# Attention and feed-forward on one core: output product five units behind, weights two pieces an iteration, interleaved tables, a mean in column groups, and a later test

## The chip, the cores and the metric

The kernel runs on one core of a Trainium2 chip. The metric is the device time of one execution in microseconds (us), the median of several. A profile's *span* is the time from the first to the last instruction; here it lies some 1.7 to 2.2 us below the time of the same execution.

## The reference

A linear attention with decay (RWKV-5) over 4 batches, 8 heads, 768 steps, head size 48, followed by a feed-forward block with SoLU and a layer norm. Cut to what matters:

```python
# attention, for every step t
y[:, :, t] = einsum('bhd,bhde->bhe', rt, state + (u*kt) vt)
state = w * state + kt vt
# feed-forward on x = y as (3072, 384); w_in is 384 x 1024, w_out 1024 x 384
h    = x @ w_in
solu = h * softmax(h)
ln   = (solu - mean(solu)) / sqrt(var(solu) + 1e-6) * g_ln
out  = ln @ w_out
```

The feed-forward weights arrive as 64-bit floats; the kernel converts them to 32-bit in 14 pieces (6 of `w_in`, 8 of `w_out`).

## The kernel before

The work is cut into 24 units of 128 rows, (batch, chunk). One loop runs a software pipeline over them, in an order that the program fixes for every engine. In iteration `i` unit `i + 2` is turned (`tr`, `tk`), unit `i + 1` gets its scores (`at`), unit `i` its attention output and state update (`y`, `kv`), unit `i - 2` its first feed-forward product (`h`) and SoLU (`solu`), and unit `l` is turned (`t`) and multiplied with `w_out` (`o`). Before the change `l = i - 5`, that is `LA, LO = 2, 3`.

Instead of subtracting the mean from every row, the kernel subtracts the column mean from `w_out` once (`centre`), so `o` of the first unit must wait for all of `w_out`. While it runs it tests that the decays and the sums of Exp lie in a safe range; a small matrix product (`n_ps`) adds the results up, and a branch at the end redoes all in another way if the test failed.

Short names in what follows: `rku` is the product of r, k and u, and `own` its sum per head; `kp` is k weighted with the decay; rT, kT and lnT are the turned r, k and `solu` after their copy out of PSUM (the memory that TensorE writes; the kernel shares it out in banks), and xT is the copy of the attention output `y`.

```python
    for j in range(7):                                   # tables, one after the other
        nc.vector.tensor_mul(pw[:, 0, j + 1], pw[:, 0, j], pw[:, 0, j])
    double(0)                                            # 7 products: decay backward
    ...                                                  # kdec from it, then
    nc.vector.reciprocal(out=pw[:, 1], in_=pw[:, 0])
    nc.vector.tensor_copy(out=fore[:, :, T - 1 : T], in_=pw[:, 1, 0].unsqueeze(2))
    double(1)                                            # 7 products: its inverse
    ...
    def column_mean(fs):                                 # mean over the rows of w_out
        for f in fs:
            nc.tensor.matmul(mean[0], ones, w_out_sb[:, f, :], start=(f == 0), stop=(f == KF - 1), ...)
            if f == KF - 1:
                nc.scalar.copy(out=mean_sb, in_=mean[0])
    ...
    conversions = {-2: 1, -1: 1, 0: 2, 1: 2, 2: 3, 3: 3, 4: 2}
    for i in range(-2, N + LA + LO):
        j, l = i - LA, i - LA - LO
        ...                     # turn_r, sum_own, turn_k of unit i + 2
        ...                     # convert_d of the last pieces; convert_a, convert_b of this iteration's
        if i + 3 < N:
            decay_k(i + 3)      # kp, on GpSimd
        for p in now:
            convert_c(p)        # adds the low words, on GpSimd
        if i + 3 < N:
            weigh(i + 3, nc.gpsimd)   # rku
        ...
        if 0 <= j < N:
            ffn_in(j)           # h, Exp
        if l == 0:
            column_mean(fs); centre(...) ; turn_ln(l)
        if 0 <= i + 1 < N:
            scores(i + 1)       # at, masked copy
        if 0 <= j < N:
            unit(j)             # solu, Square, statistics
        if i == N + LA - 1:
            check_sums()        # n_ps
        if i + 2 < N:
            diagonal(i + 2)     # AT, on ScalarE
        ...                     # t, o, then y, kv, xT of unit i
```

## Time and profile before

| | before |
|---|---|
| median time | 432.87 us (432.8 to 433.84) |
| span of the profile | 431.2 us |
| TensorE busy | 400.3 us, 93% |
| end of the first `solu` | 51.57 us |
| `h` of iteration 6 starts | 98.96 us in the timeline (99.13 in the chain) |
| a steady iteration, from `h` to `h` | 16.08 us, all of it TensorE work |

In the profile PE is TensorE, PEld its weight load, DVE VectorE, ACT ScalarE, POOL GpSimd. A line of a timeline has the start, the duration, engine, source line, operation, output and inputs, shapes and count, and in brackets how long the engine stood idle before it and what ended that. The chain of work that ended last has start, duration and what ran. The prediction below shows the lines of before and how to read them.

### The profile page before, as it was taken

The numbers are of one execution on the slowest core, as the hardware profiler recorded it, in microseconds if no ns is written. First come the engines' busy times: TensorE is split into PE (matmuls) and PEld (weight loads), VectorE is DVE, ScalarE is ACT, GpSimd is POOL, SyncE is SP. The second block draws the span as 40 slices with busy tenths as digits, with TensorE's granted clock in tenths as the row PEclk, the third lists the DMA queues.
The fourth block names the chain that finished last, engine by engine and source line by source line (L and its number), as shares of the span: only waits on it lengthen the run. The fifth ranks groups of instructions, "written<-read, shape, count | busy, mean of one in ns | idle before, by whom it ended". The sixth has DMA issues, their size and how long they took to land.

```text
span 431.2 us, 7237 instructions
## 1 busy us (share of the span) xinstructions
PE 400.3 (93%) x2871; PEld 252.9 (59%) x2871; DVE 158.2 (37%) x303; ACT 181.3 (42%) x423; POOL 145.2 (34%) x220
## 2 busy tenths in 40 slices
PE   2689598999999999999999999999999999998895
PEld 1576355565665665665665665665665665554562
DVE  6787965373224226224224224233233132111200
ACT  1776268633552552552552452452452452323211
POOL 4587644763513513513414414414413011001100
PEclk9998889999999999999999999999999999999898
DMA  8998990003403303303303303302300000000011
GB/s 167 282 215 188 184 117 5 2 0 75 74 6 69 74 14 63 73 17 60 73 20 56 73 22 55 73 24 52 73 20 1 20 20 1 20 20 19 2 38 43
DMA packets 81593, 25.93 MB, mean 60 GB/s; under 512 B 76557, under 2 KB 79758, under 8 KB 81550
## 3 DMA queue, kind: packets, MB, share of 16 engines
q1 hardware_dynamic: 81406, 25.18, 29.1%
q8 instruction: 24, 0.39, 0.4%
q10 hardware_dynamic: 144, 0.20, 0.1%
q14 instruction: 19, 0.16, 0.1%
HBM read 20.65 MB, written 4.72 MB: 59 GB/s over the span
## 4 chain that ended last, share of the span: by engine, by line
PE 79%; DVE 10%; ACT 4%; POOL 2%; issue 2%; DMA 1%; ACTq 0%; POOLq 0%; DVEq 0%; SPq 0%
PE o_ps L817 29%; PE h_ps L774 25%; PE y_ps L744 7%; PE t_ps L806 5%; PE at L716 5%; PE kv_ps L760 4%; DVE ma L524 2%; PE tk_ps L705 2%; PE tr_ps L697 2%; DVE ma L526 2%; ACT AT L691 2%; DVE mag L520 1%; DVE tab L575 1%; DVE w_out_sb L663 1%; POOL rku L680 1%
## 5 line engine op out<-in xcount | busy, mean ns | idle before, releaser
L774 PE MATMUL h_ps<-w_in_sb,xT 128*128 128x512 f32 x288 | 130.1, 602 | 5.1 <-DVE solu L786 5.1
L817 PE MATMUL o_ps<-w_out_sb,lnT 128*128 128x384 f32 x384 | 130.8, 495 | 1.0 <-DVE lnT L808 1.0
L817 PEld LDWEIGHTS o_ps<-w_out_sb,lnT 128*128 128x128 f32 x384 | 72.0, 192 | 49.6 <-issue 3.3
L774 PEld LDWEIGHTS h_ps<-w_in_sb,xT 128*128 128x128 f32 x288 | 53.8, 194 | 64.2 <-issue 64.2
L719 DVE COPY_PREDICATED AT<-later,at 128x512 f32<-128x512 uint32 x48 | 32.1, 721 | 94.8 <-ACT e L777 94.8
L777 ACT ACTIVATE e<-h_ps 128x1024 f32<-128x1024 f32 x24 | 24.5, 1023 | 93.8 <-PE h_ps L774 93.8
L691 ACT ACTIVATE AT<-ident,own 128x128 f32<-128x128 f32 x192 | 58.4, 386 | 4.5 <-DVE own L685 4.5
L789 ACT ACTIVATE sq<-solu 128x1024 f32<-128x1024 f32 x24 | 25.4, 1057 | 76.6 <-DVE solu L786 76.6
L791 POOL TENSOR_TENSOR st<-st 128x1 f32<-128x1 f32 x24 | 4.6, 193 | 149.9 <-DVE solu L786 149.9
L716 PEld LDWEIGHTS at<-rT,kT 48*128 48x128 f32 x384 | 25.7, 199 | 19.0 <-issue 15.7
L763 DVE TENSOR_TENSOR state<-kv_ps,state 128x384 f32<-128x384 f32 x16 | 8.9, 558 | 74.5 <-PE kv_ps L760 74.5
L764 POOL TENSOR_TENSOR state<-state,wt 128x384 f32<-128x384 f32 x16 | 16.1, 1006 | 51.1 <-DVE state L763 51.1
L716 PE MATMUL at<-rT,kT 48*128 48x128 f32 x384 | 30.8, 298 | 2.5 <-DVE AT L719 2.4
L674 POOL TENSOR_TENSOR kp<-kpad,kdec 128x512 f32<-128x512 f32 x24 | 31.2, 1302 | 5.5 <-ACT kdec L591 5.4
L786 DVE SCALAR_TENSOR_TENSOR solu<-h_ps,st,e 128x1024 f32<-128x1024 f32 x24 | 30.8, 1284 | 1.0
L808 DVE COPY lnT<-t_ps 128x512 f32<-128x512 f32 x24 | 16.4, 684 | 30.2 <-PE t_ps L806 30.0
L744 PE MATMUL y_ps<-AT,vt 128*32 128x128 f32 x768 | 27.2, 285 | 0.0
L806 PE MATMUL t_ps<-ident,solu 128*128 128x128 f32 x192 | 25.6, 277 | 0.2 <-ACT xT L756 0.2
L706 ACT COPY kT<-tk_ps 128x512 f32<-128x512 f32 x24 | 14.0, 583 | 24.9 <-PE tk_ps L705 24.8
L760 PE MATMUL kv_ps<-vt,kp 128*128 128x96 f32 x160 | 24.2, 298 | 0.0
L681 POOL TENSOR_TENSOR rku<-rku,rpad 128x384 f32<-128x384 f32 x23 | 22.9, 997 | 1.8
L820 ACT ACTIVATE o<-o_ps,st 128x384 f32<-128x384 f32 x24 | 13.6, 566 | 23.6 <-PE o_ps L817 15.1
(77 smaller groups left out, 375.0 us busy)
## 6 DMA issues: line engine op xcount, KB each, us to landing
kpad<-in_k_dram SPq DMA_DIRECT2D x24, 192.0 KB, 3.4
rpad<-in_r_dram SPq DMA_DIRECT2D x24, 192.0 KB, 4.1
vt<-in_v_dram SPq DMA_DIRECT2D x24, 192.0 KB, 4.0
out_dram<-o SPq DMA_DIRECT2D x24, 192.0 KB, 2.0
raw<-in_moe_w_in_dram SPq DMA_DIRECT2D x6, 512.0 KB, 5.6
raw<-in_moe_w_out_dram SPq DMA_DIRECT2D x8, 384.0 KB, 3.4
u_bc<-in_u_dram ACTq DMA_DIRECT2D x1, 192.0 KB, 3.7
wq<-in_w_dram SPq DMA_DIRECT2D x1, 1.5 KB
```

The lines of the kernel that those rows point to most:

```text
L674: nc.gpsimd.tensor_mul(X["kp"].rearrange("p h d -> p (h d)"), kpads[i % NLD].rearrange("p h d -> p (h d)"), kdec.rearrange("p a d -> p (a ...
L691: nc.scalar.activation(out=AT[:, h, :], in_=ident, func=ACT.Copy, scale=X["own"][:, h])
L716: nc.tensor.matmul(pss[q][:, a, :], X["kT"][rows, a, :], X["rT"][rows, a, :], start=True, stop=True)
L719: nc.vector.copy_predicated(A4[:, :, q, :], later.to_broadcast([128, HP, T]), pss[q])
L744: nc.tensor.matmul(y_ps[32 * g : 32 * g + 32, j, :], lhsT, rhs, start=(g not in opened), stop=stop, skip_group_check=True)
L760: nc.tensor.matmul(kv_ps[:, a], pair(X["kp"], a), vt[:, 2 * a : 2 * a + 2, 0:D], start=True, stop=True)
L774: nc.tensor.matmul(h_ps[:, ts(n, NX)], X["xT"][:, j, :], w_in_sb[:, j, ts(n, NX)], start=(j == 0), stop=(j == KD - 1))
L777: nc.scalar.activation(out=e, in_=h_ps, func=ACT.Exp, accum_out=sums[:, i : i + 1])
L786: nc.vector.scalar_tensor_tensor(out=solu, in0=X["h"], scalar=rs, in1=X["e"], op0=ALU.mult, op1=ALU.mult, accum_out=tot)
L789: nc.scalar.activation(out=sq, in_=solu, func=ACT.Square, accum_out=ss)
L806: nc.tensor.transpose(t_ps[:, f, :], X["solu"][:, ts(4 * g + f, 128)], ident)
L817: nc.tensor.matmul(o_ps, X["lnT"][:, f, :], w_out_sb[:, f, :], start=(f == 0), stop=(f == KF - 1))
```

## The change

Its intent: to empty the head of the kernel, where TensorE waits for the weight conversion, and the tail, where it waits for the test. The output product falls two units further behind, so that the 14 pieces can be spread at two an iteration; the two tables grow together; `rku` of the first units stands ahead of the weight addition on GpSimd; the column mean is summed in four groups of 32 columns, which needs a second product to add the groups; Square writes over `e`; and the test goes to the very end. The diff, cut to its core:

```diff
-    LA, LO = 2, 3
+    LA, LO = 2, 5
...
-    for j in range(7):
-        nc.vector.tensor_mul(pw[:, 0, j + 1], pw[:, 0, j], pw[:, 0, j])
-    double(0)
+    for j in range(8):
+        if j < 7:
+            nc.vector.tensor_mul(pw[:, 0, j + 1], pw[:, 0, j], pw[:, 0, j])
+            nc.vector.reciprocal(out=pw[:, 1, j], in_=pw[:, 0, j])
+        if j == 0:
+            nc.vector.tensor_copy(out=fore[:, :, T - 1 : T], in_=pw[:, 1, 0].unsqueeze(2))
+        else:
+            n = 1 << (j - 1)
+            nc.vector.tensor_mul(tab[:, :, :, T - 2 * n : T - n], tab[:, :, :, T - n : T],
+                                 pw[:, :, j - 1].unsqueeze(3).to_broadcast([128, 2, HP, n]))
...
+            nc.tensor.matmul(mean[0][ts(f % 4, 32), :], part[:, 0:32], w_out_sb[:, f, :],
+                             start=(f < 4), stop=(f >= KF - 4), skip_group_check=True)
+
+    def column_mean():
+        nc.scalar.copy(out=mean_sb, in_=mean[0])
+        ps = psM.tile([128, dm], F32, tag="m", name="mean_ps2")
+        nc.tensor.matmul(ps, part, mean_sb, start=True, stop=True)
+        nc.scalar.activation(out=mean_sb, in_=ps, func=ACT.Copy, scale=32.0 / dff)
...
-    conversions = {-2: 1, -1: 1, 0: 2, 1: 2, 2: 3, 3: 3, 4: 2}
+    conversions = {-2: 1, -1: 1, 0: 2, 1: 2, 2: 2, 3: 2, 4: 2, 5: 2}
...
             decay_k(i + 3)
+            if i < 0:
+                weigh(i + 3, nc.gpsimd)
         for p in now:
             convert_c(p)
-        if i + 3 < N:
+        if 0 <= i and i + 3 < N:
             weigh(i + 3, nc.gpsimd)
...
+        column_sums(fs)         # behind scores(i + 1)
...
-        if i == N + LA - 1:
-            check_sums()
+        if l == N - 1:          # ahead of the last output product
+            check_sums()
...
+        if 7 in fs:             # last thing in iteration 6
+            column_mean()
             for f in range(KF):
                 centre(f, nc.vector if f % 2 == 0 else nc.gpsimd)
```

Rings of `solu` and of statistics are larger to match the lag.

More of the change, by code (lines that the diff above doesn't have):

```diff
@@ L570, in direct_path @@
     nc.vector.memset(back[:, :, T - 1 : T], 1.0)
-    def double(x):
-        for j in range(7):
-            n = 1 << j
-            nc.vector.tensor_mul(tab[:, x, :, T - 2 * n : T - n], tab[:, x, :, T - n : T],
-                                 pw[:, x, j].unsqueeze(2).to_broadcast([128, HP, n]))
     wd_ps = psM.tile([128, HP], F32, tag="m", name="wd_ps")
@@ L581, in direct_path @@
                             op0=ALU.max, op1=ALU.min)
-    for j in range(7):
-        nc.vector.tensor_mul(pw[:, 0, j + 1], pw[:, 0, j], pw[:, 0, j])
-    double(0)
+    for j in range(8):
[8 more added lines that the diff above has]
+                                 pw[:, :, j - 1].unsqueeze(3).to_broadcast([128, 2, HP, n]))
     kdec = const.tile([128, HP, 128], F32, name="kdec")
@@ L591, in direct_path @@
     nc.scalar.copy(out=kdec, in_=kd_ps)
-    nc.vector.reciprocal(out=pw[:, 1], in_=pw[:, 0])
-    nc.vector.tensor_copy(out=fore[:, :, T - 1 : T], in_=pw[:, 1, 0].unsqueeze(2))
-    double(1)
     later = const.tile([128, 1, T], U32, name="later")
@@ L641, in check_sums, with column_sums @@
         n_ps = psM.tile([1, 1], F32, tag="m", name="n_ps")
-        nc.tensor.matmul(n_ps, low, ones[:, 0:1], start=True, stop=True)
-        nc.vector.tensor_scalar(out=bad, in0=n_ps, scalar1=all_ok, scalar2=127.5 / dff,
+        nc.tensor.matmul(n_ps, low, part[:, 0:1], start=True, stop=True)
+        nc.vector.tensor_scalar(out=bad, in0=n_ps, scalar1=all_ok, scalar2=127.5 / 32,
                                 op0=ALU.mult, op1=ALU.is_lt)
-    ones = const.tile([128, 128], F32, name="ones")
+    part = const.tile([128, 128], F32, name="part")
     mean_sb = const.tile([128, dm], F32, name="mean_sb")
-    nc.gpsimd.memset(ones, 1.0 / dff)
+    nc.gpsimd.memset(part, 1.0 / 32)
     mean = []
-    def column_mean(fs):
-        if not mean:
+    def column_sums(fs):
+        if fs and not mean:
             mean.append(psM.tile([128, dm], F32, tag="m", name="mean_ps"))
         for f in fs:
-            nc.tensor.matmul(mean[0], ones, w_out_sb[:, f, :], start=(f == 0), stop=(f == KF - 1),
-                             skip_group_check=True)
-            if f == KF - 1:
-                nc.scalar.copy(out=mean_sb, in_=mean[0])
+            nc.tensor.matmul(mean[0][ts(f % 4, 32), :], part[:, 0:32], w_out_sb[:, f, :],
[5 more added lines that the diff above has]
+        nc.scalar.activation(out=mean_sb, in_=ps, func=ACT.Copy, scale=32.0 / dff)
     def centre(f, engine):
@@ L781, in unit @@
         X = live[i]
-        st = small.tile([128, 8], F32, name="st")
+        st = small.tile([128, 8], F32, name="st", bufs=LO + 3)
         rs, tot, ss, sqm, var, rstd = (st[:, n : n + 1] for n in range(6))
@@ L787, in unit @@
                                        op0=ALU.mult, op1=ALU.mult, accum_out=tot)
-        sq = fpool.tile([128, dff], F32, name="sq", bufs=1)
-        nc.scalar.activation(out=sq, in_=solu, func=ACT.Square, accum_out=ss)
+        nc.scalar.activation(out=X["e"], in_=solu, func=ACT.Square, accum_out=ss)
         nc.gpsimd.tensor_mul(sqm, tot, tot)
@@ L830, in direct_path @@
         j, l = i - LA, i - LA - LO
-        drain = i >= N + LA - 1
         if i == 0:
@@ L861, in direct_path @@
             check_range()
-        if 0 < l and not i > N + LA - 1:
+        if 0 <= l and not i > N + LA - 1:
             turn_ln(l)
@@ L865, in direct_path @@
             ffn_in(j)
-        if l == 0:
-            column_mean(fs)
+        if 0 <= i + 1 < N:
+            scores(i + 1)
+        column_sums(fs)
+        if 0 <= j < N:
+            unit(j)
+        if i + 2 < N:
+            diagonal(i + 2)
+        if i >= N + LA - 1 and l + 1 < N:
+            turn_ln(l + 1)
+        if l == N - 1:
+            check_sums()
+        if 0 <= l:
+            ffn_out(l)
+        if 0 <= i < N:
+            finish(i)
+        if 7 in fs:
+            column_mean()
             for f in range(KF):
                 centre(f, nc.vector if f % 2 == 0 else nc.gpsimd)
-            turn_ln(l)
-        if 0 <= i + 1 < N:
-            scores(i + 1)
-        if 0 <= j < N:
-            unit(j)
-        if i == N + LA - 1:
-            check_sums()
-        if i + 2 < N:
-            diagonal(i + 2)
-        if drain and l + 1 < N:
-            turn_ln(l + 1)
-        if l <= 0 <= i:
-            finish(i)
-        if 0 <= l:
-            ffn_out(l)
-        if 0 < l and i < N:
-            finish(i)
-        if l < 0 and fs:
-            column_mean(fs)
     return bad
```

## The prediction

> **What bounds the kernel now.** I read the page's engine row first, then the chain that ended last, then the timelines of TensorE, VectorE, ScalarE and GpSimd over the first 100 us and of all engines over the last 45 us.
>
> The page says that TensorE is the bound on average, and the chain of work that ended last says where it is not:
>
> ```profile
> PE 400.3 (93%) x2871; PEld 252.9 (59%) x2871; DVE 158.2 (37%) x303; ACT 181.3 (42%) x423; POOL 145.2 (34%) x220
> PE 79%; DVE 10%; ACT 4%; POOL 2%; issue 2%; DMA 1%; ACTq 0%; POOLq 0%; DVEq 0%; SPq 0%
> ```
>
> In order of time, the chain is one block of TensorE work per iteration from 98 us on. A steady iteration is tr + tk 0.88, t 0.87, h 5.15, at 1.09, o 5.36, y 1.67, kv 1.06 = 16.08 us, and the h blocks start at 99.13, 115.20, 131.28: exactly that sum, so nothing off TensorE matters there. Before 98 us the chain runs through other engines. One lap of it (chain in order of time; start, us, what):
>
> ```profile
> 65.92 1.15 ACT sq L789 x2
> 67.07 2.33 ACT AT L691 x8
> 69.77 0.48 ACT kT L706
> 70.25 1.53 ACT w_out_sb L541 x3
> 71.77 0.45 ACT mag L510
> 73.03 0.56 DVE ma L526
> ...
> 75.73 0.92 issue
> ```
>
> The reader is to see a ring: Square (sq), diagonal, turned k, three weight scalings, first magnitude on ScalarE; then the conversion of the pieces, the masked copy and solu on VectorE; then Square again. From solu's end to solu's end (65.82 to 78.17 in the VectorE timeline) it takes 12.35 us, more than the 10 us or so of TensorE work in such an iteration. The lap before, with three pieces to convert, took 14.25.
>
> TensorE waits in two large holes (TensorE timeline; idle time and releaser in brackets):
>
> ```profile
> 51.73 7.83 PE L774 MATMUL h_ps<-w_in_sb,xT 128*128 128x512 f32 x12 [5.11 <-DVE solu L786]
> 66.91 5.32 PE L774 MATMUL h_ps<-w_in_sb,xT 128*128 128x512 f32 x12
> 400.74 0.19 PE L642 MATMUL n_ps<-ones,low 128*1 128x1 f32 x2 [3.47 <-DVE low L640]
> 400.86 1.50 PE L806 MATMUL t_ps<-ident,solu 128*128 128x128 f32 x8
> 402.16 6.64 PE L817 MATMUL o_ps<-w_out_sb,lnT 128*128 128x384 f32 x16
> ```
>
> After each hole the same twelve or sixteen instructions run slower: 7.83 instead of 5.32, and 1.50 + 6.64 instead of 1.04 + 5.33 us.
>
> **What the Trainium skill says.** "TensorE: Matmul & The Clock Gate", Part 1: TensorE drops to half its clock after an idle window of about 3.4 us and needs about that long of work to come back. The trace agrees: holes of 5.11 and 3.47 us are followed by 2.5 and 1.8 us of lost time, holes of about 1 us by none. Same page, Part 3: matmuls that write to different 32-column groups run at the same time. The trace agrees in the y product: 56 instructions of 128 columns take 1.67 us, 30 ns each, where a full-width transpose takes 0.44/4 = 109 ns. "SBUF — State Buffer", Who interferes with whom: VectorE and GpSimd share a port pair; an instruction of VectorE with two SBUF inputs, or in a two-port mode, waits for the whole GpSimd instruction. The trace agrees: the same shift of a w_out piece takes 0.36 us alone and 1.06 us beside GpSimd's addition of the piece before, and a table step at 9.35 us takes 1.50 us beside the first kp product.
>
> **The change, part by part.**
>
> *Test of sums last.* Its one-column product stood between h of the last unit and the turns, so TensorE waited for VectorE. It now comes before the last output product, when every sum is long known. Removed: 3.47 us idle and the slow clock after it, 0.46 + 1.3: **5.2 us**, all at the end where TensorE is the only path. Five behind instead of three puts five t+o pairs (6.03 us each) behind the last h, so nothing there waits. What follows the last o product (5.0 us) stays.
>
> *Tables interleaved.* On VectorE 4.33 to 7.34 us made the back table, and to 10.85 the other. Now both end together: 14 steps of 0.18, a copy of 0.2, seven products of double width, which by the sizes of the form view sum to some 2.3 us: end at 9.4. The kdec transposes, and with them the first kp, move from 9.30 to about 11.3: 2.0 later. Against this, rku of units 1 and 2 stands before the weight addition on GpSimd, whose wait made VectorE idle 2.89, 1.68 us before `own`. But then GpSimd runs back to back and VectorE's conversions meet it at the shared port, some 1 us each time. Walking both queues through to `own` of unit 2 (24.78 before) I get 23.0 without port waits and 25.0 with all of them. I take **0.4 us gained**, uncertain by 1.5.
>
> *Two pieces an iteration.* Iteration 2 converts two pieces instead of three: VectorE's solu ends 1.96 us sooner (the third piece: 0.35 + 1.05 + 0.56). It ends at 51.57 − 1.96 − 0.4 = 49.2. Iterations 3, 4, 5 each convert two and scale two: a lap of 12.35 less one scaling of 0.51 = 11.84 us. The fifth solu-end (iteration 5) is thus at 49.2 + 3 × 11.84 = 84.7, and h of iteration 6 starts 1.08 later (as 78.17 to 79.25 now), at **85.8**. Before, that h started at 99.13, with 5.36 + 2 × 0.87 = 7.1 us of output work already done. Net: 99.13 − 85.8 − 7.1 = **6.2 us ahead**, of which 2.4 were counted above (conversion and tables).
>
> *Mean in four column groups.* The sums come two at a time, so only two groups overlap: 2 × 0.33 = 0.65 us per iteration, four times, instead of 5.2 us in all. Three of these lie inside the laps that TensorE does not bound. The last (0.65) and the second product (0.65) are paid.
>
> *The mean's second step, a new wait.* In iteration 6 TensorE does h 5.25, at 1.09, sums 0.65, y 1.67, kv 1.06 and would be done 10.8 us after the fifth solu-end. The second product stands next on its queue and needs ScalarE's copy of the sums, which stands behind Exp (to 7.6), VectorE's copies and solu (7.5 to 10.2), Square (11.4), diagonal (13.8), xT (14.15) and itself (14.6). TensorE idles **3.9 us**. That is about the length of the hole that brought the slow clock at the end, so it may cost 2 us more; I give that two chances in three, **1.3 us**. The centring (4.4 us on VectorE, 5.2 on GpSimd) then has the 8 us of tr, tk, t, h, at before the first o product and is hidden.
>
> **Sum.** 6.2 (head) − 0.65 − 0.65 − 3.9 − 1.3 + 5.2 (end) = 4.9 us gained; 431.2 − 4.9 = 426.3 of span. The three times lie 1.6 above the span, so about **427.9 us**, 1.1% less than 432.87. As a check from the other side: from the start of iteration 7 the TensorE work, by the durations of the chain, is 239.1 (iterations 7 to 21) + 14.3 + 13.0 + 11.3 + 12.1 + 24.1 + 5.2 = 319.0, plus 5.0 at the end and 0.8 of small gaps; iteration 7 starts at 84.7 + 14.7 + 0.65 + 1.3 = 101.3, and the sum is 426.1.
>
> The larger ring of solu tiles, the larger ring of statistics and Square written over e cost nothing that I can see: same instructions, sizes and engines.
>
> **Rivals.** (1) *The mean waits less, or the clock stays up.* If ScalarE reaches the copy sooner, or the hole stays under a window, the 3.9 + 1.3 shrink to 2 or so, and the reordered head gains its full 2 us: 423 to 424, just past 2%. For it: the slow clock depends on where the hole falls. Against: the order on ScalarE is fixed, and xT precedes the copy. (2) *The head gives it all back.* Kp starts 2 us later, and GpSimd and VectorE block each other in the first three iterations, so that h of iteration 2 comes 2 us later and not sooner: 430 to 431. For it: the 1.06 and 1.50 us waits above. Against: VectorE now idles there, 2.89, 1.68 and 1.21 us, so it has something to lose the waits in. (3) *The laps do not shrink,* because TensorE takes ScalarE's place as the bound: its work in iterations 4 and 5 is 10.5 us, with 1.1 of waiting for solu, close to 11.84. Then each lap is up to 0.5 longer and the time 429. (4) *Only the end counts* and the head merely shifts: 427.7.
>
> **Range and chances.** The end's 5.2 us is safe to half a microsecond. The head varies by 1.5, three laps by 0.5 each, the hole and the clock by 2: together about 3. Nothing here makes it slower than before unless head and hole both go wrong. Faster by over 2% needs 424.3, which needs rival 1 almost whole. So 424.0 to 431.0, with chances 0.19 for faster, 0.79 for within 2%, 0.02 for slower.
>
> **What would show it.** Right: no idle before n_ps and 5.2 us for each of the last o products; table products ending near 9.4 and the first kp near 11.3; laps of some 11.8 us from solu to solu in iterations 3 to 5; sums in pairs at 0.65 us; one hole of some 4 us before the second mean product, released by ScalarE's copy, with slow transposes after it; then 16.08 us an iteration. Wrong: a hole before the first o product (centring not hidden), a steady iteration of other length, or a lap bound by TensorE or a DMA.

## The result, and the profile after

The changed kernel takes 427.27 us (426.55 to 427.52, four runs) against 432.84 of four runs of the kernel before on the same chip; the ratio is 0.9871, 95% interval 0.9841 to 0.9901: 1.3% faster, outside the noise. The span is 425.5 us. The prediction said 427.9 us and 426.3 of span.

The page's row of engines and the shares of the chain:

```profile
PE 396.0 (93%) x2873; PEld 250.3 (59%) x2873; DVE 157.5 (37%) x302; ACT 181.6 (43%) x424; POOL 146.7 (34%) x220
PE 78%; DVE 9%; ACT 8%; POOL 2%; issue 2%; DMA 1%; ACTq 0%; POOLq 0%
```

TensorE is busy for 4.3 us less, some of which is slow clock and not work, and idle for 1.4 us less (30.9 to 29.5), so its share stays 93%. In the chain ScalarE doubled, from 4% to 8%. The timeline of TensorE after shows where its waits are now:

```profile
46.58 7.08 PE L774 MATMUL h_ps<-w_in_sb,xT 128*128 128x512 f32 x12 [3.99 <-DVE solu L786]
...
96.67 1.65 PE L659 MATMUL mean_ps<-mean_sb,part 128*128 128x384 f32 x2 [3.84 <-ACT mean_sb L657]
98.11 1.06 PE L697 MATMUL tr_ps<-ident,rpad 128*128 128x128 f32 x4
99.82 1.86 PE L805 MATMUL t_ps<-ident,solu 128*128 128x128 f32 x8
101.52 5.32 PE L774 MATMUL h_ps<-w_in_sb,xT 128*128 128x512 f32 x12
...
413.86 0.19 PE L638 MATMUL n_ps<-part,low 128*1 128x1 f32 x2
```

The hole before `n_ps` is gone (no bracket). A new one of 3.84 us stands before the mean's second product, released by ScalarE's copy of the sums, and the transposes after it run at half rate: 1.06 for four where they take 0.60 later. The granted clock, as a share of full speed, is 0.50 from 94.7 to 101.5 us and 1.00 on both sides. The chain of waits shows what ScalarE was doing:

```profile
91.01 1.30 DVE solu L786 x2
...
92.39 1.15 ACT e L788 x2
93.54 2.34 ACT AT L691 x8
95.88 0.36 ACT xT L756
96.24 0.38 ACT mean_sb L657
96.63 0.04 issue
96.67 1.65 PE mean_ps L659 x2
```

From `solu` on, ScalarE does Square, the diagonal and xT before it comes to the copy. The sums that the copy reads were complete at about 90.2 us.

The ledger between the two traces, in us: `h` of iteration 6 starts at 83.06 instead of 98.96, with 7.1 of output work still to do, so 8.8 ahead. The fourth pair of sums and the second product cost 1.4, the hole 3.84, the slow clock after it 2.35. The end gains 5.2 (hole and slow clock around `n_ps`), and the stretch from the last output copy to the end is 0.9 longer. 8.8 − 1.4 − 3.84 − 2.35 + 5.2 − 0.9 = 5.5, and the spans differ by 5.7; the two output pairs that moved to the end are a little denser there (6.03 us each instead of 6.23).

### The profile page after: what moved, and what is told of

Its sections match the earlier page's. It is cut to its first block, busy times and chain, and to the rows that moved or that the text cites. A ratio compares the mean times of both kernels' runs of the same rounds, so it can differ in the third digit from the quotient of the medians.

```text
span 425.5 us, 7222 instructions
## 1 busy us (share of the span) xinstructions
PE 396.0 (93%) x2873; PEld 250.3 (59%) x2873; DVE 157.5 (37%) x302; ACT 181.6 (43%) x424; POOL 146.7 (34%) x220
## 4 chain that ended last, share of the span: by engine, by line
PE 78%; DVE 9%; ACT 8%; POOL 2%; issue 2%; DMA 1%; ACTq 0%; POOLq 0%
PE o_ps L816 30%; PE h_ps L774 24%; PE y_ps L744 7%; PE t_ps L805 5%; PE at L716 4%; ACT AT L691 3%; PE kv_ps L760 3%; DVE ma L524 2%; PE tk_ps L705 2%; DVE ma L526 2%; PE tr_ps L697 2%; DVE AT L719 1%; DVE mag L520 1%; DVE solu L786 1%; ACT e L788 1%
## 5 line engine op out<-in xcount | busy, mean ns | idle before, releaser
L816 PE MATMUL o_ps<-w_out_sb,lnT 128*128 128x384 f32 x384 | 129.5, 491 | 0.0
L816 PEld LDWEIGHTS o_ps<-w_out_sb,lnT 128*128 128x128 f32 x384 | 71.2, 190 | 47.5 <-issue 1.0
L788 ACT ACTIVATE e<-solu 128x1024 f32<-128x1024 f32 x24 | 25.4, 1057 | 71.0 <-DVE solu L786 71.0
L764 POOL TENSOR_TENSOR state<-state,wt 128x384 f32<-128x384 f32 x16 | 16.1, 1006 | 47.5 <-DVE state L763 47.5
L805 PEld LDWEIGHTS t_ps<-ident,solu 128*128 128x128 f32 x192 | 22.6, 144 | 2.7 <-issue 2.0
```

The lines of the kernel that those rows point to most:

```text
L788: nc.scalar.activation(out=X["e"], in_=solu, func=ACT.Square, accum_out=ss)
L805: nc.tensor.transpose(t_ps[:, f, :], X["solu"][:, ts(4 * g + f, 128)], ident)
L816: nc.tensor.matmul(o_ps, X["lnT"][:, f, :], w_out_sb[:, f, :], start=(f == 0), stop=(f == KF - 1))
```

## The experiments

Twelve kernels ran, all of them correct; every one is the changed kernel with one thing altered (e8 and e13 have two, e11 three). Each was timed in three rounds beside the kernel before. A span is that of the one profiled run. That Square writes over `e`, and that the rings are larger, was not undone by itself.

### e1: the test where it was

```diff
-        if l == N - 1:
-            check_sums()
+        if i == N + LA - 1:        # behind unit(j)
+            check_sums()
```

> The changed kernel with the test of sums put back where it was (after solu of the last unit), all else as changed. Theory of the prediction: the 3.5 us hole before n_ps returns, with slow t and o products after it (1.8 us): 5.2 us more than the changed kernel, less up to 0.9 because the changed kernel's stretch after its last output copy is 0.9 us longer than before (span 425.5 + 4.3 to 5.2 = 429.8 to 430.7). Rival: in the tail five t+o pairs stand behind it now, and the hole costs nothing or is taken up elsewhere: 425.5.

Measured: 432.59 us, ratio 0.9979, span 431.6. The timeline of TensorE at the end:

```profile
387.61 0.19 PE L638 MATMUL n_ps<-part,low 128*1 128x1 f32 x2 [3.40 <-DVE low L636]
387.73 1.17 PE L805 MATMUL t_ps<-ident,solu 128*128 128x128 f32 x8
388.69 6.98 PE L816 MATMUL o_ps<-w_out_sb,lnT 128*128 128x384 f32 x16
```

The hole is back at 3.40 us, and the first `t` and `o` after it take 8.15 together where later pairs take 6.37 (1.04 and 5.33): 5.2 us in all, as the prediction had it. (The rest of the 6.1 us is 0.45 in the head and 0.5 in the stretch after the last copy; the profiled run is the slowest of the four, and the others have spans of 430.5 to 430.9.) The late test alone is worth nearly the whole gain of the change; the head and the mean nearly cancel.

### e2 and e3: the tables and the order of rku, each undone

e2 puts back the code of the tables before. e3:

```diff
             decay_k(i + 3)
-            if i < 0:
-                weigh(i + 3, nc.gpsimd)
         for p in now:
             convert_c(p)
-        if 0 <= i and i + 3 < N:
+        if i + 3 < N:
             weigh(i + 3, nc.gpsimd)
```

> The changed kernel with the two tables made one after the other, as before. The prediction said that interleaving delays the first kp by 2.0 us (it came 0.46 sooner). Theory A: interleaving helps, because neighbouring instructions are independent and overlap (one starts every 0.07 to 0.09 us instead of 0.18): undone, the second table ends near 10.5 us instead of 6.96, the first rT starts 1.6 us later, and the first solu ends 1 to 1.6 us later than 46.43; span 426.5 to 427.1. Theory B: the order of rku alone gave the head its gain, and the tables are hidden behind kp: span within 0.5 us of 425.5.

> The changed kernel with rku of the first units behind the weight addition again, as before. Theory A (rku order carries most of the head's gain): own of unit 1 comes at about 18 us again instead of 15.65, and the first solu ends 1.5 to 2.5 us later than 46.43; span 427 to 428. Theory B (tables carry it): within 0.5 us of 425.5.

Measured: e2 428.32 us, ratio 0.9880, span 426.8; e3 430.34 us, ratio 0.9923, span 428.5. The interval of e2's ratio (0.9854 to 0.9907) does not part it from the changed kernel, so the trace decides: the first `solu` ends at 47.89 in e2 and 48.96 in e3, against 46.43. Both parts count, the order of `rku` more (2.5 us) than the tables (1.5 us), and neither theory holds alone. Some 0.3 to 0.6 of each can be chance: `w` landed 0.22 and 0.28 us later in these runs, and in e1 and e7 to e11, whose tables and order of `rku` are unaltered but whose `w` landed as late, the first `solu` ends at 46.7 to 47.0.

The tables are the step that the prediction had the wrong way round. VectorE's timeline, first of the kernel before:

```profile
4.33 1.34 DVE L583 TENSOR_TENSOR pw<-pw 128x4 f32<-128x4 f32 x7
5.58 1.84 DVE L575 TENSOR_TENSOR tab<-tab,pw 128x4 f32<-128x4 f32 x7
...
7.92 2.92 DVE L575 TENSOR_TENSOR tab<-tab,pw 128x4 f32<-128x4 f32 x7
```

then of the changed kernel:

```profile
4.40 0.15 DVE L577 TENSOR_TENSOR pw<-pw 128x4 f32<-128x4 f32 x1
4.47 0.17 DVE L578 RECIPROCAL pw<-pw 128x4 f32<-128x4 f32 x1
4.56 0.14 DVE L583 TENSOR_TENSOR tab<-tab,pw 128x8 f32<-128x8 f32 x1
...
5.84 1.12 DVE L583 TENSOR_TENSOR tab<-tab,pw 128x256 f32<-128x256 f32 x2
```

Before, seven products each of which reads the last one's result take 1.25 us from the first start to the next row, 0.18 each. After, neighbours are of three kinds and start every 0.06 to 0.09 us, though each is still 0.15 long: they overlap. Both tables are done at 6.96 us instead of 7.42 and 10.84. They are also done before GpSimd's first `kp` (8.84 us); before the change the last table product ran beside it and took 1.49 us, where one of the same size took 0.42 alone. What tables and order do together shows at `own` of unit 2 on VectorE, before and after the change:

```profile
24.78 0.55 DVE L685 TENSOR_REDUCE own<-rku 128x8 f32<-128x384 f32 x1 [1.68 <-POOL rku L681]
```

```profile
21.48 0.53 DVE L685 TENSOR_REDUCE own<-rku 128x8 f32<-128x384 f32 x1
```

### e9: the test one output product sooner

```diff
-        if l == N - 1:
+        if l == N - 2:
```

> The changed kernel with the test of sums one output product sooner (6 us), where all sums are long known too. From the last output copy to the end takes 5.9 us in the changed kernel and 5.0 in the one before, where the test's result was known 25 us before the end. Theory: the result is loaded by every engine for the branch at the end, and known late it holds up the fetching of what follows: 0.9 us less, span 424.6. Rival: the stretch after the last store varies by chance with the fetches: no change within 0.5 us on the mean of the rounds.

Measured: 428.77 us, ratio 0.9886, span 427.6: nothing gained, 1.5 us are lost. The stretch from the start of the last output copy to the end is 6.0 us, as in the changed kernel (5.9). Over all fourteen profiles it lies between 4.9 and 6.5 us; the longest is e1's, where the test is earliest. So the rival holds: its length is not the test's doing. What sets it stays open. The run also showed why the place in the change is the right one:

```profile
410.71 0.19 PE L638 MATMUL n_ps<-part,low 128*1 128x1 f32 x2 [1.09 <-DVE low L636]
```

One iteration sooner the test stands behind that iteration's copy of a turned unit on VectorE, which itself waits for TensorE, and so TensorE waits again. Of the 2.1 us of span 1.1 are this wait, 0.6 a later head (a load of `r` landed late for iteration 2, 1.11 us of wait).

### e5: three pieces an iteration again

```diff
-    conversions = {-2: 1, -1: 1, 0: 2, 1: 2, 2: 2, 3: 2, 4: 2, 5: 2}
+    conversions = {-2: 1, -1: 1, 0: 2, 1: 2, 2: 3, 3: 3, 4: 2}
```

> The changed kernel with three pieces in iterations 2 and 3 again and two in iteration 4. Theory of the ring: the first solu ends 1.96 us later (48.4), the laps are 14.25 and 12.35 instead of three of 11.85, the mean falls into iteration 5 and opens the same hole there, and an iteration without weight work and without output product (about 10 us of TensorE) follows: iteration 7 about 3 us later, span 428.5. Rival: the number of conversions in all is the same, so only their order changes and the span stays within 1 us of 425.5.

Measured: 431.26 us, ratio 0.9964, span 428.3. The first `solu` ends at 48.30 (48.4 expected), the laps take 14.3 and 12.4 (14.25 and 12.35), and the hole before the second product is 3.83. `h` of iteration 7 starts 2.35 us later than in the changed kernel (3 expected). The ring that the prediction describes is the bound of the head. (The profiled run is the fastest of the four; the others have spans of 429.2 to 430.2, so the expected 428.5 was up to 1.7 too low.)

### e13: six units behind

```diff
-    LA, LO = 2, 5
+    LA, LO = 2, 6
```

(and the ring of `solu` kept at seven tiles; with eight, as e12, the kernel did not fit in memory and was refused when built.)

> The changed kernel with the output product six behind instead of five, and the ring of solu tiles kept at seven so that it fits. Theory: the lag in itself gains nothing; what counts is that the output product starts no sooner than the centred weights. One more t+o pair goes from iteration 7 (107.9 now) to the end, where it is as dense (6.03 us), and TensorE has enough other work in iteration 7: span 425.5 within 0.5. Rival: the lag is what fills the end or empties the head, and one step more moves the time by more than 1 us either way.

Measured: 426.35 us, ratio 0.9854 (0.9814 to 0.9894), span 424.1. The last output copy starts at 419.24 instead of 419.58; the other 1.1 us of span is the stretch after it, which varies anyway. The span lies 1.4 below the changed kernel's, where 0.5 was expected, but the intervals of the two ratios overlap, so nothing clear of noise is gained. A further lag gains next to nothing. That the lag is the room that the two-piece spread needs follows from the program's order; two pieces with the old lag were not run.

### e4: the mean in one step

```diff
-            nc.tensor.matmul(mean[0][ts(f % 4, 32), :], part[:, 0:32], w_out_sb[:, f, :],
-                             start=(f < 4), stop=(f >= KF - 4), skip_group_check=True)
+            nc.tensor.matmul(mean[0], part, w_out_sb[:, f, :], start=(f == 0), stop=(f == KF - 1), ...)
...
-        nc.scalar.copy(out=mean_sb, in_=mean[0])
-        (second product and copy)
+        nc.scalar.activation(out=mean_sb, in_=mean[0], func=ACT.Copy, scale=32.0 / dff)
```

> The changed kernel with the mean in one step again: eight full-width products into one sum, one copy, at the same place in the order. Theory of the prediction: the column groups save TensorE 0.65 us in iteration 6 only, and their second product opens the hole; with one step there is no TensorE instruction that waits for ScalarE's copy, so the hole (3.84) and the slow clock after it (2.45) go, the sums cost 0.65 more there, and the centring, now behind the same late copy at about 96.6, holds up the first o product by some 1.4 us: 5 us less, span 420.5. Rival: the hole is merely moved, to the first o product that waits for the centring: span within 1 us of 425.5.

Measured: 423.41 us, ratio 0.9780 (0.9753 to 0.9807), span 421.6. The hole and the slow clock are gone, with the copy at the same late place (96.24). So the column groups, meant to save TensorE time, cost the changed kernel 3.9 us of span where they stand. It is 1.1 short of what was expected. Of this 0.3 is a longer stretch after the last copy and 0.1 the head; the rest is that the wait expected before the first `o` (1.4) did not come and somewhat more was lost before `h`, where nothing was expected:

```profile
96.39 1.09 PE L802 MATMUL t_ps<-ident,solu 128*128 128x128 f32 x8 [1.21 <-ACT xT L753]
97.33 5.32 PE L771 MATMUL h_ps<-w_in_sb,xT 128*128 128x512 f32 x12
```

`t` needs a PSUM bank. By the kernel's text the four banks of that pool are then held by `y` until xT is copied, by `tr` until VectorE gets to rT behind the centring, by `tk` and by the sums; the trace names xT. The first `o` follows `at` without a gap.

### e6 and e10: work for TensorE in the hole

```diff
+        for _ in range(28):      # 13 in e10
+            nc.tensor.matmul(ps[:, 0:128], ident, ident, start=True, stop=True)
         nc.tensor.matmul(ps, part, mean_sb, start=True, stop=True)
```

The filler writes the bank that the true product then overwrites.

> The changed kernel with 28 idle 128-column products of the identity (3 us) into the second mean's own bank ahead of it, so that TensorE has work in the hole and nothing else changes. Theory: the hole itself stays (the second product still waits for ScalarE's copy until about 96.7), but the clock stays up and the second mean product, tr, tk and t after it run at full rate: 2.45 us less, span 423.0. Rival: the slow products after the hole are not the clock's doing but the waits': span 425.5.

> The filler of the hole again, with 13 idle products instead of 28: the first try showed that each takes 0.22 us (6.2 us in all, 2.7 us longer than the hole), while what followed ran at full rate. 13 take 2.9 us and end inside the hole of 3.84. Theory: the second mean product still starts at 96.7, and from there to h takes 2.4 us instead of 4.85: span 423.0. Rival: with a shorter filler the clock drops all the same: 425.5.

Measured: e6 427.50 us, span 425.6, no gain; e10 425.24 us, ratio 0.9811, span 424.1. e6's filler was mis-sized:

```profile
93.20 6.44 PE L660 MATMUL mean_ps<-ident 128*128 128x128 f32 x56
99.48 0.81 PE L661 MATMUL mean_ps<-mean_sb,part 128*128 128x384 f32 x2
```

28 products took 6.2 us, 0.22 each, twice what a transpose of the same size takes (0.44 for four), and delayed the true product by 2.3 (it would have started at about 97.2, 0.5 after the start of the copy at 96.69, as in the changed kernel; the 2.7 in the text of e10 is too much). In e10 they end inside the hole:

```profile
93.31 3.09 PE L660 MATMUL mean_ps<-ident 128*128 128x128 f32 x26
97.31 0.91 PE L661 MATMUL mean_ps<-mean_sb,part 128*128 128x384 f32 x2 [0.91 <-ACT mean_sb L657]
98.06 0.60 PE L699 MATMUL tr_ps<-ident,rpad 128*128 128x128 f32 x4
```

The true product starts no sooner, and from it to `h` takes 2.50 us instead of 4.85. The granted clock is 1.00 throughout. The slow stretch is thus the clock's, set by the idle time before, and costs 2.35 us; the hole costs the rest. The span is 1.4 us lower and not 2.4, because `h` of iteration 6 started 0.65 later in that run (83.71 against 83.06) and the end stretch was 0.3 longer. (The profiled run is the slowest of the four; the others have spans of 423.3 to 423.5.)

### e7 and e8: the copy of the sums ahead of Square

```diff
         column_sums(fs)
+        if 7 in fs:
+            column_mean()
         if 0 <= j < N:
             unit(j)
...
         if 7 in fs:
-            column_mean()
             for f in range(KF):
                 centre(...)
```

e8 is this together with the one-step mean of e4.

> The changed kernel with both steps of the mean moved ahead: right behind the sums, before Square of the unit, on all engines; the centring stays at the end of the iteration. Theory: ScalarE stands idle there (89.5 to 92.4), so TensorE waits only 0.7 us for the copy, y and kv follow, the hole and the slow clock go: 5.7 us less, span 419.8, and the first o product waits for nothing. Rival: ScalarE's copies ahead of Square delay diagonal and xT, and the hole comes back before y of the next iteration: span above 423.

> The changed kernel with the mean in one step (eight full-width products, one copy) and that copy moved ahead, right behind the sums. It joins the two runs that each took the hole away. Theory: no TensorE instruction waits for the copy, so y starts 1.0 us sooner than in the run with both steps early; but the t products of the next iteration still wait for the bank that xT frees at about 96.4, so h starts at about 97 as there: span 420.5 to 421.2. Rival: y was what held xT, and the whole 1.0 us comes through: 420.1.

Measured: e7 423.13 us, ratio 0.9772 (0.9745 to 0.9799), span 421.1; e8 423.82 us, ratio 0.9784, span 422.0. TensorE in e7:

```profile
91.15 0.91 PE L659 MATMUL mean_ps<-mean_sb,part 128*128 128x384 f32 x2 [0.60 <-ACT mean_sb L657]
...
96.52 0.66 PE L805 MATMUL t_ps<-ident,solu 128*128 128x128 f32 x4 [0.41 <-ACT xT L756]
97.01 5.32 PE L774 MATMUL h_ps<-w_in_sb,xT 128*128 128x512 f32 x12
```

The hole shrinks from 3.84 to 0.60 with the column groups kept: it was the place of the copy in ScalarE's order that opened it. The same bank holds `t` up again, 0.41 us here and 1.27 in e8. e7's span is 1.3 above the expected 419.8: 0.6 went before `h` of iteration 7 with this wait, 0.3 is a later `h` of iteration 6, 0.1 the stretch after the last copy. e8 came out 0.8 above the upper end of what was expected. Its `h` of iteration 6 starts at 84.21 (83.37 in e7), 1.87 us after `solu` instead of the usual 1.1. In that run the slow `h` of iteration 3 was long (7.77 us), as in e7, but with the full-width sums it takes 3.16 us from the first of them to `kv`, where the groups take 2.30 in the changed kernel, and that left TensorE no slack in the laps. That is what the column groups are good for. It was not tested by itself, but five traces agree. From `solu` to this `h` it takes 1.09 us in e7 and e10 (groups, slow `h` 7.74 and 8.18), 1.16 in e4 (full-width sums, slow `h` only 7.08), and 1.87 and 1.97 in e8 and e11 (full-width sums, 7.77 and 8.17). How long the slow `h` takes is nothing that the edits explain: in e8 the granted clock fell inside the hole (0.50 from 44.9 to 51.7), in e4 and the changed kernel after it (47.5 to 50.9, 46.9 to 50.3); see the closing list.

### e11: the version that the runs point to

The one-step mean of e4, the early copy of e7, and the centring behind rT and `own` of iteration 7:

```diff
             turn_k(i + 2)
+        if i == 7:
+            for f in range(KF):
+                centre(f, nc.vector if f % 2 == 0 else nc.gpsimd)
```

> The version that the runs point to: mean in one step, copied right behind the sums, and the centring moved behind rT and own of the next iteration, so that rT frees its bank before the centring and t need not wait for xT. Theory: h of iteration 7 starts at about 95.3 instead of 97.0, the centring ends at about 99.5 on VectorE and 101 on GpSimd, before the first o product at 101.5: span 419.4, 1.4% less than the changed kernel. Rival: the centring, 1 us later, now holds up lnT and the first o product: span 421.

Measured: 421.86 us, ratio 0.9731 (0.9706 to 0.9757), span 420.7: 2.7% faster than the kernel before, and below every other run.

```profile
95.90 1.20 PE L802 MATMUL t_ps<-ident,solu 128*128 128x128 f32 x8
96.93 5.32 PE L771 MATMUL h_ps<-w_in_sb,xT 128*128 128x512 f32 x12
```

`t` waits for nothing. The span missed the expected 419.4 by 1.3, nearly all of it before: `h` of iteration 6 started at 84.56 (83.37 in e7), for the reason given under e8 (the slow `h` took 8.17 us). The profiled run is the slowest of the four; the others have spans of 419.7 to 420.4. Column groups with the copy early and the centring late might take that back; it was not run.

| run | what is altered | median us | ratio to before | span us |
|---|---|---|---|---|
| changed kernel | | 427.27 | 0.9871 | 425.5 |
| e1 | test early | 432.59 | 0.9979 | 431.6 |
| e2 | old tables | 428.32 | 0.9880 | 426.8 |
| e3 | old order of rku | 430.34 | 0.9923 | 428.5 |
| e4 | mean in one step | 423.41 | 0.9780 | 421.6 |
| e5 | three pieces | 431.26 | 0.9964 | 428.3 |
| e6 | hole filled, 28 | 427.50 | 0.9874 | 425.6 |
| e7 | mean's copies early | 423.13 | 0.9772 | 421.1 |
| e8 | e4 and e7 | 423.82 | 0.9784 | 422.0 |
| e9 | test one sooner | 428.77 | 0.9886 | 427.6 |
| e10 | hole filled, 13 | 425.24 | 0.9811 | 424.1 |
| e11 | e4, e7, centring later | 421.86 | 0.9731 | 420.7 |
| e12 | lag six, ring of eight | not built | | |
| e13 | lag six, ring of seven | 426.35 | 0.9854 | 424.1 |

## Why the prediction was right or wrong

The time, 427.27 us, fell 0.6 below the predicted 427.9 and inside the range. That it came so close is partly luck: one term was mis-sized by 2.7 us one way, two by 1.1 and 0.9 the other way.

- **The end: right.** 5.2 us predicted; e1 gives back 5.2 (hole 3.40, slow `t` and `o` 1.8). That the stretch after the last product "stays" at 5.0 was too firm: it varies between runs by more than a microsecond, and took 0.9 here.
- **The laps: right.** 11.84 predicted; from the trace after the first `solu` ends at 46.43 and the fourth (the prediction miscounts it as the fifth) at 81.98, three laps of 11.85. e5 shows that a third piece costs what the ring says.
- **Tables and order of rku: wrong, a term of the sum.** The prediction took 0.4 us for both, uncertain by 1.5; the first `solu` ended 3.2 us sooner than 51.57 less the 1.96 of the third piece (0.3 of it is a load that landed sooner). The failed step is "14 steps of 0.18": that is the spacing of products that wait for each other, and independent neighbours start every 0.06 to 0.09. So the tables were done at 6.96 and not 9.4, and the first `kp` came 0.46 sooner (0.3 of it the load), not 2.0 later. `own` of unit 2 starts at 21.48 and not at about 24.4. The slowed instructions that the prediction feared are there (up to 1.53 us), but VectorE no longer idles 2.89 and 1.68 us before `own`; that the one fell into the room of the other is read from the timelines. e2 and e3 put 1.5 and 2.5 us on the two parts when one is undone. Alone, against 49.61 (51.57 − 1.96), the order gains 1.7 and the tables 0.65, so each is worth more beside the other.
- **Two pieces: right** (1.96 us less in iteration 2, by e5 1.87 more when undone).
- **The hole before the second mean product: right**, 3.9 predicted and 3.84 measured, with the releaser named. Its consequence too: e7 moves the copy and the hole is gone, e4 removes the second product and it is gone.
- **The clock after the hole: mis-sized.** It was entered as two chances in three of 2 us, 1.3; it came, in every run with that hole, and costs 2.35 by e10. The size is partly chance: in e13 the granted clock was 0.50 for 3.4 us instead of 6.8, which loses about 1.7 (an estimate, half of 3.4).
- **Centring hidden: right.** No wait before the first `o` in the changed kernel.
- **Rivals.** Rival 1 (less waiting at the mean) is not what happened, but e4 and e7 show that its size, 423 to 424, was right. Rival 2 was wrong in sign. Rival 3, TensorE as the bound of the laps, does not show in the changed kernel. It shows at the last `h` of the head in e8 and e11, and where the slow `h` of iteration 3 took 8.17 us or more (e6, e10, e11) the lap with it takes 12.2 to 12.3. Rival 4's number, 427.7, was close for a wrong reason: head and mean do not vanish, they cancel.

By terms: the span was predicted at 426.3. The head came 2.7 sooner (`h` of iteration 6 at 83.06 instead of 85.8), the clock cost 1.1 more and the end stretch 0.9 more: 425.6, and 425.5 was measured. (The net of 6.2 for the head sets 99.13, a start from the chain, against starts from the timeline, where that `h` starts at 98.96; on one scale it is 6.0.)

## What to carry to other kernels

When orders are fixed, a product that waits for a copy stands where that copy stands in the *other* engine's queue: before adding a second step to save array time, look what the copying engine has in front of it, and place the copy where that engine idles. Undo a change part by part even when its sum comes out as predicted: here one part cost 3.9 us while the whole gained 5.7, and removing it and moving two pieces of code doubled the gain. A table of small steps on VectorE is worth interleaving with a second one, because only dependent neighbours pay the full latency (0.18 us against 0.06 to 0.09 here).

## What the Trainium skill lacked or had wrong

- **"TensorE: Matmul & The Clock Gate", Part 1 (The HAM clock gate)** says that the clock follows free-running windows of 3.413 us. The traces agree: in the changed kernel the granted clock falls to 0.50 at 46.89 us, returns at 50.30, falls at 94.68 and returns at 101.50, steps of 1, 13 and 2 times 3.41. What the page lacks is the price of one hole. In the traces the slow stretch after a hole is one or two such windows, 3.4 or 6.8 us. After one and the same hole of 4.0 us the same `h` takes from 6.82 to 8.33 us in eleven runs (5.32 at full rate), so 1.5 to 3.0 us are lost. Holes of 3.15 us (in e5) to 5.95 us all brought the slow clock.
- **The same page, Part 4 (PE-mode transpose)** says that the full clock does not engage for transposes. Here four transposes take 0.44 us from start to start when TensorE has been busy and 0.85 after a hole: they follow the clock like any product. (No run shows whether transposes alone would bring the full clock.)
- **The same page, Terms (xbus)** calls the transpose mode four times faster for 32-bit floats, without saying than what. Here a 128-column product of the identity takes 0.22 us and a transpose of the same size 0.11: twice.
- **"VectorE: DVE Perf Modes", The DRAIN you can't avoid** says that the next instruction does not start until the pipeline has emptied. Here small independent neighbours of 0.15 us start every 0.06 to 0.09 us, and dependent ones every 0.18. (The same section adds that an instruction that is not held starts earlier, without times.)
- No page gives the stretch from the last output copy to the end of the span as one time: 4.9 to 6.5 us over fourteen profiles. Of it 0.6 is the copy and about 1.9 the landing of the last store; the rest, and why it varies, stays open.
